# Column tiles for the dense work that follows a visit of values

## The chip, the cores and the metric

The kernel runs on one core of a Trainium2 chip. The metric is the device time of one execution in microseconds. Before the change the median of three runs is 562.47 us (562.46 to 562.88).

## What is computed

Two layers of attention with a memory (A), each followed by a feed-forward block (B), on 2048 tokens of width 640, in bf16:

```
x = x + A(layernorm(x));  x = x + B(layernorm(x))      # twice, the same weights
A:  q, k, v = x @ wq, x @ wk, x @ wv                   # 32 heads of 20, 4 segments of 512 tokens
    for each segment s:
        p     = softmax(q_s k_s^T / sqrt(20) + causal mask)
        a_dot = p @ v_s
        a_mem = phi(q_s) @ M / (phi(q_s) @ z + 1e-6)   # phi(t) = t + 1 where t > 0, else exp(t)
        o_s   = g * a_mem + (1 - g) * a_dot            # g = sigmoid(beta), per head
        M, z += phi(k_s)^T @ v_s, sum phi(k_s)
    out = o @ wo
B:  out = relu(x @ w1) @ w2                            # 640 to 1728 to 640
```

## The kernel before

The kernel is written by a planner. Every piece of work is a stream: a Python generator that yields operations (scores, exponentials, causal masks, values, transposes, projections, the memory's reads and writes, the feed-forward block, loads). An operation names its engine, the time that the planner holds that engine for it, the semaphores it waits for and the PSUM bank or buffer that it needs. `Sched.run` takes from all streams the operation that can start first by its own clock, with priorities, and appends it to the list of its engine; each engine then works through its list in that order. Everything is unrolled. The plan is made 48 times with slightly different prices for a switch of TensorE (around 97 ns), and the plan with the shortest modelled time is emitted.

TensorE works in three forms. The planner calls them modes and adds 97 ns (`SWITCH_NS`) where an operation's mode differs from that of the one before.

- "rows", the scores (L1114): four heads at once, each head's 20 features in a row tile of 32 partitions, 4 or 8 matmuls in each of the two score buffers. ScalarE takes the exponential of a buffer in one instruction of 1024 columns (L1166), GpSimd cuts the diagonal blocks (L1178).
- "cols", the values: `apply` (L1257) multiplies the probabilities of one group of four heads with the values. Four column tiles of 32 stand side by side, one for each head, and four steps of 512, 384, 256 and 128 columns follow each other, so 16 matmuls, called a visit here. There are 60 of them; four more groups (m of 2 and 3) are worked token by token, in the whole-array form (L1208). The last 64 hidden features of a feed-forward block (`ffn_last`, L1405) also have this mode; they use two column tiles of 64, for two halves of the tokens, and 10 matmuls.
- "full", all else: dense matmuls through the helper `group` (L651 the first of a group, L654 the others): the projections of q, k (512 columns, one chunk of 128 features) and v (320), the output projection (320), the first (512) and second (320) matmul of the feed-forward block. The memory's read (L1007, groups of three matmuls of 147 or 84 columns) and its write (L1058, 147 or 168 columns) are in this form too.

The scores pace the attention: between two rounds of them, some 2 to 3 us apart, the planner fills TensorE's list with a visit where one is due, and with whatever dense work is ready. An operation of mode "cols" that would follow whole-array work is held back by up to 4 us (`JOIN_NS`), so that it may come right behind a round of scores. Scores, visits and dense work wait for ScalarE, VectorE, GpSimd and the DMA queues by semaphores; SP issues the transfers, among them the transposes.

Of the kernel before, what the change touches and what calls it, by code (L numbers as in the profile page):

```python
# [16 lines left out]
DFF = 1728  # L17
# [96 lines left out]
class Op:  # L114
# [1 line left out]

    def __init__(self, alts, waits, dma=None, acq=None, urgent=False, take=(), mode="full"):
        self.alts = alts  # L120
        self.mode = mode
# [55 lines left out]
class Sched:  # L177
# [72 lines left out]
    def _pick(self, slots):  # L250
        return min((s for s in slots if s.free), default=None,
                   key=lambda s: max([self.at(t) for t in s.tks], default=0.0))

    def _alts(self, op):
        res = []
        waits = op.waits
        if op.acq is not None:
            s = self._pick(op.acq)
            if s is None:
                return res  # L260
            waits = waits + s.tks
        for k, (e, hold, fns, tail) in enumerate(op.alts):
            m = PE_MARGIN if e == "pe" else 0.0
            if e == "pe" and op.mode != self.pe_mode:
                hold = hold + self.switch
            start = max([self.at(t) + SEM_NS + m for t in waits], default=0.0)
            start = max(self.free[e], start)
            res.append((start + hold, start, k, e))
        return res

    def run(self):
        while True:
# [50 lines left out]
                    str(getattr(st[2], "key", None) or [s.name for s in st[2].slots][:2]) for st in stuck))  # L323
            _, st, end, start, k, op = best
            e, hold, fns, tail = op.alts[k]
            waits, slot = op.waits, None
            for s in op.take:
                s.free = False
# [4 lines left out]
                fns = [(lambda eng, fn=fn, slot=slot: fn(eng, slot), mark) for fn, mark in fns]  # L333
            if e == "pe":
                self.keep_busy(op, start)
                if op.mode != self.pe_mode:
                    hold = hold + SWITCH_NS
            self.P.waits(e, waits)
            self.free[e] = end
            if e == "pe":  # L340
                self.pe_mode = op.mode
            if op.dma is not None:
                tk = self.P.dma(e, fns[0][0], op.dma)
                self.dma_free = max(self.dma_free, start + 300.0) + tail[1]
# [40 lines left out]
        return max(t.values())  # L385


def pe(ns, fns, waits=(), acq=None, take=(), mode="full"):
    return Op([("pe", ns, fns, 190.0)], waits, acq=acq, take=take, mode=mode)


def mm_ns(n):
# [26 lines left out]
def plan(switch, sb, sem_, psum, dram, A_x, A_wq, A_wk, A_wv, A_wo, A_beta, B_x, B_w1, B_w2, out):  # L419
# [224 lines left out]
    def group(slots, n, mms, waits):  # L644

        bk = tk = None
        last = len(mms) - 1
        for k, (a, b, *w) in enumerate(mms):
            w = list(w[0]) if w else []
            if k == 0:  # L650
                bk, tk = yield pe(mm_ns(n), [(lambda e, bk, a=a, b=b: e.matmul(  # L651
                    bk.ap[:, 0:n] if len(b.shape) == 2 else bk.ap[:, 0:n].rearrange("p (i n) -> p i n", n=128), a, b, start=True, stop=(last == 0)), last == 0)], list(waits) + w, acq=slots)
            else:
                tk = yield pe(mm_ns(n), [(lambda e, k=k, a=a, b=b, bk=bk: e.matmul(  # L654
                    bk.ap[:, 0:n] if len(b.shape) == 2 else bk.ap[:, 0:n].rearrange("p (i n) -> p i n", n=128), a, b, start=False, stop=(k == last)), k == last)], w)
        return bk, tk


# [335 lines left out]
    def mem_read(hb):  # L994
        def f(a, s):
            if s == 0:
                return
            phi = yield Need("phi", a, s)
            bdt = yield Need("BD", a, s - 1)
            yield Acq([OMS[hb]])  # L1000
            wr = []
            lst = [(c, max(CH_H0[c], 16 * hb), min(CH_H1[c], 16 * hb + 16)) for c in range(FC)]
            lst = [x for x in lst if x[1] < x[2]]
            for i in range(NJ):
                fns = []
                for z, (c, h0, h1) in enumerate(lst):
                    fns.append((lambda e, bk, c=c, h0=h0, h1=h1, z=z, i=i: e.matmul(  # L1007
                        bk.ap[:, (h0 - 16 * hb) * 21:(h1 - 16 * hb) * 21],
                        STGS[sx(a, s)][:, c, 1, i * 128:(i + 1) * 128],
                        BD[:, CH_OFF[c] + (h0 - CH_H0[c]) * 21:CH_OFF[c] + (h1 - CH_H0[c]) * 21],  # L1010
                        start=(z == 0), stop=True, skip_group_check=True), z == len(lst) - 1))
                bk, tk = yield pe(60.0 * len(lst), fns, phi + bdt, acq=MISC[:1])
# [31 lines left out]
    def mem_write(a, s):  # L1044
        mg = yield Need("maskg")
        if s < NSEG - 1:
            vt = yield Need("v", a, s)
            upd = []
            lastd = None
            for p, cs in enumerate(PARTS):  # L1050
                pht = yield Need("phkT", a, s, p)
                o0 = CH_OFF[cs[0]]
                w = CH_OFF[cs[-1] + 1] - o0
                bk = None
                for i in range(NJ):
                    fns = []
                    for c in cs:
                        fns.append((lambda e, b=None, c=c, i=i, o0=o0, st=(i == 0 and c == cs[0]), bk=bk: e.matmul(  # L1058
                            (b or bk).ap[:, CH_OFF[c] - o0:CH_OFF[c + 1] - o0], phk[:, c, i, :],
                            VAUG[vx(a, s)][:, i, CH_H0[c]:CH_H1[c], :].rearrange("p h e -> p (h e)"),  # L1060
                            start=st, stop=True, skip_group_check=True), i == NJ - 1 and c == cs[-1]))
                    if i == 0:
                        bk, lastd = yield pe(66.0 * len(cs), fns, pht + vt, acq=MISC)
                    else:
                        lastd = yield pe(66.0 * len(cs), fns)
# [330 lines left out]
    def ffn_last(b, s):  # L1396
# [5 lines left out]
        fns = []  # L1402
        for k in range(FC):
            for z in range(2):
                fns.append((lambda e, bk, k=k, z=z: e.matmul(  # L1405
                    bk.ap[64 * z:64 * z + 64, 0:256].rearrange("p (i n) -> p i n", n=128),
                    w1_r[:, k, NFULL * 128:DFF], feat(xt, k)[:, 2 * z:2 * z + 2],
                    start=(k == 0), stop=(k == FC - 1)), k == FC - 1 and z == 1))
# [168 lines left out]
```

## Time and profile before

| | |
|---|---|
| median of three runs | 562.47 us |
| the profiled execution: its own time | 562.46 us |
| its span, first to last instruction | 560.6 us |
| TensorE: busy, matmuls | 555.5 us (99%), 5110 |
| weight loads: busy, number | 302.6 us (54%), 5111 |
| VectorE, ScalarE: busy | 410.8 us, 409.7 us (73% each) |
| GpSimd: busy | 194.3 us (35%) |
| chain that ended last: share of TensorE | 90% |
| granted TensorE clock | 1.00 |

The groups are named by line, engine, operation, what is written and read, and the shape: `128*32 128x512` is a matmul with 128 rows and 32 columns of the array that streams 512 columns, `20*128` a row tile, `128*128` the whole array. In the order of time each row has the start, the time to the end of the last of its instructions, and the number of them (x16); instructions of neighbouring lines of the same helper are merged. TensorE's matmuls overlap, and the end of each is modelled, so distances between starts say more than the lengths of the records: a matmul of 512 columns has a record of some 380 ns, and the next one starts long before it is over.

### The profile page before, as it was taken

Reading aid. Unit: us, or ns where it says so; the run is one execution under the profiler, and the core shown is the slowest. Engines: PE = TensorE matmul, PEld = TensorE weight load, DVE = VectorE, ACT = ScalarE, POOL = GpSimd, SP = SyncE. Lnnn points to the kernel's source line nnn. Section 1 sums busy time; section 2 is a strip of 40 time slices with the busy share of each in tenths; the row PEclk is TensorE's granted clock in tenths of the full one; section 3 lists DMA queues with packets and bytes.
Section 4 is the critical chain, followed back from the end, with each engine's and each line's share of the span. In section 5 each row is a group of like instructions: output and inputs, shape, how many; then the busy total and the mean of one; then the engine's idle time right before and its main releaser. Section 6 shows DMA issues by size and latency. Waiting matters only on the chain.

```text
span 560.6 us, 12651 instructions
## 1 busy us (share of the span) xinstructions
PE 555.5 (99%) x5110; PEld 302.6 (54%) x5111; DVE 410.8 (73%) x1060; ACT 409.7 (73%) x522; POOL 194.3 (35%) x302
## 2 busy tenths in 40 slices
PE   8999999999999999999999999999999999999998
PEld 7654545545644455645356554465445654665655
DVE  5898899776998787877888987889824866651202
ACT  5799999987699779787897789877856788323140
POOL 4534344333354444344433443335401433100000
DMA  8599988741374137443373505550325510422101
GB/s 269 118 201 219 254 202 164 172 123 44 90 175 99 50 89 185 88 99 79 97 179 52 127 20 137 131 120 20 67 77 154 114 43 20 93 69 55 41 1 47
DMA packets 132219, 61.43 MB, mean 110 GB/s; under 512 B 111042, under 2 KB 122050, under 8 KB 132162
## 3 DMA queue, kind: packets, MB, share of 16 engines
q1 hardware_dynamic: 131942, 60.37, 45.7%
q8 instruction: 40, 0.66, 0.5%
q10 hardware_dynamic: 220, 0.26, 0.2%
q14 instruction: 17, 0.14, 0.1%
HBM read 20.57 MB, written 12.85 MB: 60 GB/s over the span
## 4 chain that ended last, share of the span: by engine, by line
PE 90%; DVE 8%; DMA 1%; ACT 0%; POOL 0%; issue 0%
PE ps L654 58%; PE ps L651 12%; PE ps L1114 9%; PE ps L1257 7%; DVE stats L662 2%; PE ps L1058 2%; PE ps L1007 2%; DVE x_sb L1328 1%; PE ps L1405 1%; DVE stg L827 1%; DMA x_sb<-in_A_x_dram 1%; DVE xn_tok L704 1%; DVE av L1265 0%; DVE xn_tok L716 0%; DVE mv L664 0%; ACT PT L1166 0%
## 5 line engine op out<-in xcount | busy, mean ns | idle before, releaser
L1166 ACT ACTIVATE PT<-ps 128x1024 bf16<-128x1024 f32 x320 | 310.1, 1022 | 66.1 <-PE ps L1114 64.5
L1178 POOL TENSOR_SCALAR_AFFINE_SELECT PT<-PT 128x512 bf16<-128x512 bf16 x256 | 166.3, 668 | 267.7 <-ACT PT L1166 267.7
L654 PE MATMUL ps<-w_r,hT 128*128 128x320 bf16 (+2 forms) x768 | 123.4, 299 | 0.1
L654 PE MATMUL ps<-xnT,w_r 128*128 128x512 bf16 x416 | 113.6, 379 | 0.0
L1328 DVE TENSOR_TENSOR x_sb<-x_sb,ps 128x320 bf16<-128x320 bf16 (+1 forms) x128 | 60.4, 479 | 70.2 <-PE ps L654 69.9
L654 PEld LDWEIGHTS ps<-w_r,hT 128*128 128x128 bf16 x768 | 72.2, 98 | 34.2 <-issue 6.3
L1436 ACT ACTIVATE hT<-ps 128x512 bf16<-128x512 f32 x55 | 33.0, 599 | 46.4 <-PE ps L654 46.1
L1114 PE MATMUL ps<-pad 20*128 20x384 bf16 (+3 forms) x1024 | 64.9, 301 | 0.0
L654 PEld LDWEIGHTS ps<-xnT,w_r 128*128 128x128 bf16 x416 | 39.7, 98 | 42.1 <-issue 2.9
L662 DVE BATCH_NORM_STATS2 stats<-x_sb 128x6 f32<-128x320 bf16 x126 | 55.9, 470 | 2.3 <-DMA x_sb<-in_A_x_dram 2.0
L1265 DVE CAST av<-ps 128x512 bf16<-128x512 f32 x56 | 38.3, 684 | 12.9 <-PE ps L1257 12.5
L1114 PEld LDWEIGHTS ps<-pad 20*128 20x128 bf16 x1024 | 18.2, 92 | 51.4 <-ACT PT L1166 24.2
L654 PE MATMUL ps<-wo_r,oT 128*128 128x320 bf16 x256 | 45.3, 299 | 0.0
L1434 DVE TENSOR_SCALAR hT<-ps 128x512 bf16<-128x512 f32 x49 | 33.5, 684 | 10.5 <-PE ps L654 10.0
L1257 PE MATMUL ps<-PT,v_aug 128*32 128x256 bf16 (+5 forms) x896 | 40.7, 302 | 0.0
L651 PE MATMUL ps<-xnT,w_r 128*128 128x512 bf16 x104 | 39.6, 381 | 0.0
L654 PE MATMUL ps<-wv_r,xnT 128*128 128x320 bf16 x192 | 35.8, 300 | 0.0
L654 PE MATMUL ps<-xnT,wk_r 128*128 128x512 bf16 (+1 forms) x140 | 35.5, 349 | 0.0
L676 POOL TENSOR_TENSOR rstd<-lnU,mhalf 128x2 f32<-128x2 f32 (+2 forms) x25 | 20.3, 811 | 39.9 <-DVE lnU L672 39.7
L654 PE MATMUL ps<-xnT,wq_r 128*128 128x512 bf16 (+1 forms) x140 | 33.9, 349 | 0.0
L1301 DVE TENSOR_TENSOR o_sb<-avt,rden 128x320 bf16<-128x320 bf16 x60 | 33.3, 572 | 0.7
L654 PEld LDWEIGHTS ps<-wo_r,oT 128*128 128x128 bf16 x256 | 24.8, 98 | 11.3 <-issue 1.3
(120 smaller groups left out, 686.9 us busy)
## 6 DMA issues: line engine op xcount, KB each, us to landing
pad<-scr SPq DMA_DIRECT2D x124, 80.0 KB
scr<-stg SPq DMA_DIRECT2D x34, 256.0 KB, 2.9
out_dram<-x_sb SPq DMA_DIRECT2D x15, 160.0 KB, 1.8
w_r<-in_B_w_dram SPq DMA_DIRECT2D x10, 216.0 KB, 3.3
w_r<-in_B_w_dram SPq DMA_DIRECT2D x13, 160.0 KB, 2.7
x_sb<-in_A_x_dram SPq DMA_DIRECT2D x9, 160.0 KB, 3.3
scr<-w_r SPq DMA_DIRECT2D x5, 256.0 KB, 3.5
x_sb<-in_A_x_dram SPq DMA_DIRECT2D x3, 320.0 KB, 7.3
```

The lines of the kernel that those rows point to most:

```text
L651: bk, tk = yield pe(mm_ns(n), [(lambda e, bk, a=a, b=b: e.matmul(bk.ap[:, 0:n] if len(b.shape) == 2 else bk.ap[:, 0:n].rearrange("p (i n) ...
L654: tk = yield pe(mm_ns(n), [(lambda e, k=k, a=a, b=b, bk=bk: e.matmul(bk.ap[:, 0:n] if len(b.shape) == 2 else bk.ap[:, 0:n].rearrange("p (i ...
L662: tk = yield dve(320, 1, lambda e, c2=c2: e.bn_stats(stats6[:, t, c2, :], x_sb[:, t, c2 * 320:(c2 + 1) * 320]), xt)
L1114: fns.append([(lambda e, z=z, j=j, hh=hh, N=N, o=o, sl=sl: e.matmul(ps[:, hh, o:o + N], sl.ap[32 * hh:32 * hh + DH, z, 0, 128 * j:128 * j ...
L1166: tx = yield act(1024, lambda e, dst=dst, src=src: e.activation(dst, src, ACT.Exp, scale=SCALE), sc + pw)
L1178: tm = yield pool(600.0, lambda e, reg=reg: e.affine_select(out=reg, in_=reg, pattern=[[0, 4], [1, 128]], compare_op=ALU.is_ge, fill=0.0, ...
L1257: fns.append((lambda e, bk, j=j, hh=hh, pt=pt, g=g0 + z: e.matmul(bk.ap[32 * hh:32 * hh + wide(g, hh), 128 * j:L], VAUG[vx(a, s)][:, j].re ...
L1265: te = yield evac(L, 1, lambda e, sl=sl, z=z, bk=bk: e.tensor_copy(sl.ap[:, z], bk.ap), lambda e, sl=sl, z=z, bk=bk: e.activation(sl.ap[:, ...
L1301: to = yield dve(320, 1, lambda e, dst=dst, src=src, rz=rz: e.tensor_tensor(dst, src, rz, ALU.mult), [tg] + OSB.tks)
L1328: ta = yield dve(n, 1, lambda e: e.tensor_tensor(x_sb[:, t, c0:c0 + n], x_sb[:, t, c0:c0 + n], bk.ap[:, 0:n], ALU.add), [tk] + list(waits) ...
L1434: th = yield evac(512, 1, lambda e, dc=dc, bk=bk: e.tensor_scalar(hT[:, dc, :], bk.ap[:, :], 0.0, None, ALU.max), lambda e, dc=dc, bk=bk: ...
L1436: lambda e, dc=dc, bk=bk: e.activation(hT[:, dc, :], bk.ap[:, :], ACT.Relu), [tk] + HT.tks)
```

## The change

An operation of TensorE may now carry a second list of instructions, `cols`, and a surcharge, `cols_ns`. The new method `mode_of` decides between them when the operation is placed: if TensorE is in mode "cols" and the stream of scores has not ended, an operation that has such a list is emitted as column tiles and leaves the mode as it is; otherwise it is emitted as before. Dense matmuls, the memory's reads and its writes get the list: each matmul becomes four with 32 columns of the weights each, which write the four quarters of the partitions of the same bank and stream the same columns. Only the last of the four of a group's last matmul signals its semaphore. For the planner's clock the dense matmuls keep their price, those of the memory get 45 ns more each. Transposes and the values by token have no such list. `ffn_last` always uses four column tiles of 32 in place of two of 64.

```diff
+    def mode_of(self, op):
+        return "cols" if op.cols is not None and self.pe_mode in ("cols",) and not self.streams[0][4] else op.mode
...
-            if e == "pe" and op.mode != self.pe_mode:
+            if e == "pe" and self.mode_of(op) != self.pe_mode:
                 hold = hold + self.switch
+            if e == "pe" and op.cols is not None and self.mode_of(op) != op.mode:
+                hold = hold + op.cols_ns
...
+            mode = self.mode_of(op)
+            if e == "pe" and mode != op.mode:
+                fns = op.cols
...
             if e == "pe":
-                self.pe_mode = op.mode
+                self.pe_mode = mode
...
+            def whole(e, bk, k=k, a=a, b=b, wide=wide):
+                return e.matmul(to(bk.ap, wide), a, b, start=(k == 0), stop=(k == last))
+
+            def tile(e, bk, y, k=k, a=a, b=b, wide=wide):
+                return e.matmul(to(bk.ap[32 * y:32 * y + 32], wide), a[:, 32 * y:32 * y + 32], b,
+                                start=(k == 0), stop=(k == last))
...
-                tk = yield pe(mm_ns(n), [(lambda e, k=k, a=a, b=b, bk=bk: e.matmul(
-                    bk.ap[:, 0:n] if len(b.shape) == 2 else bk.ap[:, 0:n].rearrange("p (i n) -> p i n", n=128), a, b, start=False, stop=(k == last)), k == last)], w)
+                tk = yield pe(mm_ns(n), [(lambda e, bk=bk, whole=whole: whole(e, bk), k == last)], w, cols=[
+                    (lambda e, y=y, bk=bk, tile=tile: tile(e, bk, y), k == last and y == 3) for y in range(4)])
...
+                bk, tk = yield pe(60.0 * len(lst), fns, phi + bdt, acq=MISC[:1], cols=cols, cols_ns=45.0 * len(lst))
...
+                    more = dict(cols=cols, cols_ns=45.0 * len(cs))
...
             for z in range(2):
-                fns.append((lambda e, bk, k=k, z=z: e.matmul(
-                    bk.ap[64 * z:64 * z + 64, 0:256].rearrange("p (i n) -> p i n", n=128),
-                    w1_r[:, k, NFULL * 128:DFF], feat(xt, k)[:, 2 * z:2 * z + 2],
-                    start=(k == 0), stop=(k == FC - 1)), k == FC - 1 and z == 1))
+                for y in range(2):
+                    fns.append((lambda e, bk, k=k, z=z, y=y: e.matmul(
+                        bk.ap[64 * z + 32 * y:64 * z + 32 * y + 32, 0:256].rearrange("p (i n) -> p i n", n=128),
+                        w1_r[:, k, NFULL * 128 + 32 * y:NFULL * 128 + 32 * y + 32], feat(xt, k)[:, 2 * z:2 * z + 2],
+                        start=(k == 0), stop=(k == FC - 1)), k == FC - 1 and (z, y) == (1, 1)))
```

More of the change, by code (lines that the diff above doesn't have):

```diff
@@ L114, with __init__ @@
 class Op:
-    def __init__(self, alts, waits, dma=None, acq=None, urgent=False, take=(), mode="full"):
+    def __init__(self, alts, waits, dma=None, acq=None, urgent=False, take=(), mode="full", cols=None, cols_ns=0.0):
         self.alts = alts
+        self.cols = cols
+        self.cols_ns = cols_ns
         self.mode = mode
@@ L335, in run @@
                 self.keep_busy(op, start)
-                if op.mode != self.pe_mode:
+                if mode != self.pe_mode:
                     hold = hold + SWITCH_NS
+                if mode != op.mode:
+                    hold = hold + op.cols_ns
             self.P.waits(e, waits)
@@ L385, in late, with pe @@
         return max(t.values())
-def pe(ns, fns, waits=(), acq=None, take=(), mode="full"):
-    return Op([("pe", ns, fns, 190.0)], waits, acq=acq, take=take, mode=mode)
+def pe(ns, fns, waits=(), acq=None, take=(), mode="full", cols=None, cols_ns=0.0):
+    return Op([("pe", ns, fns, 190.0)], waits, acq=acq, take=take, mode=mode, cols=cols, cols_ns=cols_ns)
 def mm_ns(n):
@@ L647, in group, with to @@
         last = len(mms) - 1
+        def to(ap, wide):
+            return ap[:, 0:n] if wide else ap[:, 0:n].rearrange("p (i n) -> p i n", n=128)
         for k, (a, b, *w) in enumerate(mms):
             w = list(w[0]) if w else []
+            wide = len(b.shape) == 2
+            def whole(e, bk, k=k, a=a, b=b, wide=wide):
[3 more added lines that the diff above has]
+                                start=(k == 0), stop=(k == last))
             if k == 0:
-                bk, tk = yield pe(mm_ns(n), [(lambda e, bk, a=a, b=b: e.matmul(
-                    bk.ap[:, 0:n] if len(b.shape) == 2 else bk.ap[:, 0:n].rearrange("p (i n) -> p i n", n=128), a, b, start=True, stop=(last == 0)), last == 0)], list(waits) + w, acq=slots)
-            else:
-                tk = yield pe(mm_ns(n), [(lambda e, k=k, a=a, b=b, bk=bk: e.matmul(
-                    bk.ap[:, 0:n] if len(b.shape) == 2 else bk.ap[:, 0:n].rearrange("p (i n) -> p i n", n=128), a, b, start=False, stop=(k == last)), k == last)], w)
+                bk, tk = yield pe(mm_ns(n), [(whole, last == 0)], list(waits) + w, acq=slots, cols=[
+                    (lambda e, bk, y=y, tile=tile: tile(e, bk, y), last == 0 and y == 3) for y in range(4)])
+            else:
+                tk = yield pe(mm_ns(n), [(lambda e, bk=bk, whole=whole: whole(e, bk), k == last)], w, cols=[
+                    (lambda e, y=y, bk=bk, tile=tile: tile(e, bk, y), k == last and y == 3) for y in range(4)])
         return bk, tk
@@ L1005, in f, with read @@
                 fns = []
-                for z, (c, h0, h1) in enumerate(lst):
[L1007 to L1012, printed above, removed]
+                cols = []
+                def read(e, bk, c, h0, h1, z, p0, p1, i=i):
+                    return e.matmul(
+                        bk.ap[p0:p1, (h0 - 16 * hb) * 21:(h1 - 16 * hb) * 21],
+                        STGS[sx(a, s)][:, c, 1, i * 128 + p0:i * 128 + p1],
+                        BD[:, CH_OFF[c] + (h0 - CH_H0[c]) * 21:CH_OFF[c] + (h1 - CH_H0[c]) * 21],
+                        start=(z == 0), stop=True, skip_group_check=True)
+                for z, (c, h0, h1) in enumerate(lst):
+                    fns.append((lambda e, bk, k=(c, h0, h1, z), read=read: read(e, bk, *k, 0, 128), z == len(lst) - 1))
+                    for y in range(4):
+                        cols.append((lambda e, bk, k=(c, h0, h1, z), read=read, y=y: read(
+                            e, bk, *k, 32 * y, 32 * y + 32), z == len(lst) - 1 and y == 3))
+                bk, tk = yield pe(60.0 * len(lst), fns, phi + bdt, acq=MISC[:1], cols=cols, cols_ns=45.0 * len(lst))
                 rm = yield Acq(RMEM[hb])
@@ L1056, in mem_write, with write @@
                     fns = []
-                    for c in cs:
[L1058 to L1061, printed above, removed]
+                    cols = []
+                    def write(e, b, c, p0, p1, i=i, o0=o0, cs=cs, bk=bk):
+                        return e.matmul(
+                            (b or bk).ap[p0:p1, CH_OFF[c] - o0:CH_OFF[c + 1] - o0], phk[:, c, i, p0:p1],
+                            VAUG[vx(a, s)][:, i, CH_H0[c]:CH_H1[c], :].rearrange("p h e -> p (h e)"),
+                            start=(i == 0 and c == cs[0]), stop=True, skip_group_check=True)
+                    for c in cs:
+                        end = i == NJ - 1 and c == cs[-1]
+                        fns.append((lambda e, b=None, c=c, write=write: write(e, b, c, 0, 128), end))
+                        for y in range(4):
+                            cols.append((lambda e, b=None, c=c, y=y, write=write: write(
+                                e, b, c, 32 * y, 32 * y + 32), end and y == 3))
+                    more = dict(cols=cols, cols_ns=45.0 * len(cs))
                     if i == 0:
-                        bk, lastd = yield pe(66.0 * len(cs), fns, pht + vt, acq=MISC)
+                        bk, lastd = yield pe(66.0 * len(cs), fns, pht + vt, acq=MISC, **more)
                     else:
-                        lastd = yield pe(66.0 * len(cs), fns)
+                        lastd = yield pe(66.0 * len(cs), fns, **more)
                 if s == 0:
```

## The prediction

> **What bounds the kernel now.** I read the page's first two parts, then the busy time by stretch, then the groups of TensorE by shape, and last the order of time around single visits of values. The page and the stretches first.
>
> ```profile
> span 560.6 us, 12651 instructions
> PE 555.5 (99%) x5110; PEld 302.6 (54%) x5111; DVE 410.8 (73%) x1060; ACT 409.7 (73%) x522; POOL 194.3 (35%) x302
> 19.47:479.00 459.53, 458.90 (x4417) 239.81 (x4416) 374.94 (x965) 380.81 (x470) 181.93 (x275) 1.00 0.50 116
> 480.00:561.00 81.00, 78.23 (x518) 47.54 (x517) 22.91 (x56) 18.07 (x31) 2.75 (x4) 1.00 0.19 49
> ```
>
> The columns of the last two are the stretch, its length, the busy time (and count) of TensorE, its weight loads, VectorE, ScalarE and GpSimd, then the granted clock, the DMA share and GB/s. From the first scores (19.47 us) to the last (479.0) TensorE lacks 459.53 - 458.90 = 0.63 us of being always busy, at clock 1.00, while ScalarE and VectorE are busy for 381 and 375 of 460 us. So in this stage the time is the length of TensorE's own list, and what shortens that list shortens the run as long as the others keep up. A busy TensorE is not one at its peak, though: the order of time shows what lies between the matmuls.
>
> ```profile
> 168.61 0.39 PE L651 MATMUL ps<-xnT,w_r 128*128 128x512 bf16 x1
> 168.84 1.03 PE L654 MATMUL ps<-xnT,w_r 128*128 128x512 bf16 x4
> ...
> 254.57 0.38 PE L654 MATMUL ps<-xnT,wk_r 128*128 128x512 bf16 x1
> 254.79 0.38 PE L651 MATMUL ps<-xnT,wq_r 128*128 128x512 bf16 x1
> 255.00 0.30 PE L651 MATMUL ps<-wo_r,oT 128*128 128x320 bf16 x1
> 255.14 0.71 PE L654 MATMUL ps<-wo_r,oT 128*128 128x320 bf16 x4
> 255.78 0.40 PE L1114 MATMUL ps<-pad 20*128 20x384 bf16 x8
> 256.11 0.73 PE L1257 MATMUL ps<-PT,v_aug 128*32 128x512 bf16 x16
> 256.77 0.31 PE L651 MATMUL ps<-wo_r,oT 128*128 128x320 bf16 x1
> 256.91 0.71 PE L654 MATMUL ps<-wo_r,oT 128*128 128x320 bf16 x4
> 257.46 0.30 PE L651 MATMUL ps<-wo_r,oT 128*128 128x320 bf16 x1
> ```
>
> The first number is the start. Whole-array matmuls follow each other at their column count: 512 columns in 0.216 us (254.57 to 254.79 to 255.00), 320 in 0.136 (256.91 to 257.46 is four), so 0.425 ns a column. Scores (L1114) use row tiles, values (L1257) four column tiles of 32, dense work the whole array. A price shows at each border. The fourth matmul of the row at 255.14 starts at 255.55 and would be through at 255.68, but the scores start at 255.78: 0.10 us. The visit of values holds 16 matmuls, four abreast of 512, 384, 256 and 128 columns, 1280 columns in all, 1280 x 0.425 = 0.544 us; it takes 256.77 - 256.11 = 0.66, again 0.12 more. And the first matmul behind a border keeps the next one waiting a little longer: 168.61, behind a visit, to 168.84 is 0.23 where the cadence is 0.216; I take 0.010.
>
> **Part 1: the switch behind a visit goes.** The groups by shape give the number of visits: the 512-column matmuls of L1257, four to a visit.
>
> ```profile
> L1257 PE MATMUL ps<-PT,v_aug 128*32 128x512 bf16 x217 | 22.4, 390 | 0.0
> L1257 PE MATMUL ps<-PT,v_aug 128*21 128x512 bf16 x7 | 2.7, 385 | 0.0
> L1257 PE MATMUL ps<-PT,w_r 128*32 128x512 bf16 x16 | 1.6, 390 | 0.0
> ```
>
> (217 + 7 + 16) / 4 = 60 visits. Reading their followers in the order of time, 59 go on to whole-array work, and two of these come after the last scores, where the new code leaves everything whole. So 57 borders go, from the first of these rows to the last:
>
> ```profile
> 29.33 0.73 PE L1257 MATMUL ps<-PT,w_r 128*32 128x512 bf16 x16
> 29.99 0.45 PE L654 MATMUL ps<-wv_r,hT 128*128 128x320 bf16 x2
> ...
> 470.81 0.73 PE L1257 MATMUL ps<-PT,v_aug 128*32 128x512 bf16 x16
> 471.47 0.39 PE L651 MATMUL ps<-xnT,w_r 128*128 128x512 bf16 x1
> ```
>
> Each saves 0.116 at the border (0.66 - 0.544) and 0.010 behind it. Two bits of this stay: the visit's own first step, behind the scores, has 0.010 as well, and I leave another 0.010 to a tiled stretch for its end, since four tiles that start one after the other also end so. 0.126 - 0.020 = 0.106, and 57 x 0.106 = 6.0 us. The border in front of the next scores stays (column tiles to row tiles now); 0.10 us is what every kind of border in these rows costs.
>
> **Part 2: the last hidden chunk.** L1405 now runs two tiles of 64 columns and becomes four of 32, the form of the values, so that it can stand behind a visit without a border.
>
> ```profile
> 169.79 0.74 PE L1405 MATMUL ps<-xnT,w_r 128*64 128x256 bf16 x10
> 170.46 0.40 PE L1114 MATMUL ps<-pad 20*128 20x512 bf16 x4
> ```
>
> Ten matmuls, two abreast, are 5 x 256 x 0.425 = 0.544 us and take 0.67; the same columns four abreast take the same (a visit has 256 in one of its steps). Of the eight such blocks five are next to work of the visit's form before scores (this is one: the rows from 168.61 stand behind a visit and run up to it) and lose one border each; one more visit stands behind dense work that an earlier visit has left in column form. 6 x 0.106 = 0.6 us.
>
> **Part 3: the dense matmuls themselves.** I count 341 of 320 columns and 269 of 512 between those 57 visits and the next scores. Each becomes four matmuls and four loads. I take +0: the visit does just this, sixteen loads of 32 columns and sixteen matmuls in 0.66 us with nothing to spare between its steps. What hides the four loads is the streaming before, 0.136 or 0.216 us. If that cover is not enough, the bound from the same rows is the 0.010 that a first matmul pays: 610 x 0.010 = 6.1 us. The lower end is 0; no row has column tiles faster than the whole array.
>
> **Part 4: the memory's matmuls.** These are short, and here four instructions in place of one can show. Behind visits stand 48 of L1007 (16 groups of three) and 31 of L1058.
>
> ```profile
> 82.65 0.34 PE L1007 MATMUL ps<-BD,w_r 128*128 128x84 bf16 x3
> 82.83 0.38 PE L638 MATMUL ps<-ident 128*128 128x128 bf16 x4
> ...
> 119.13 0.34 PE L1007 MATMUL ps<-BD,stg 128*128 128x147 bf16 x3
> 119.31 0.59 PE L654 MATMUL ps<-xnT,w_r 128*128 128x512 bf16 x2
> ...
> 231.36 0.69 PE L1058 MATMUL ps<-v_aug,phk 128*128 128x147 bf16 x8
> 231.89 0.57 PE L654 MATMUL ps<-w_r,hT 128*128 128x320 bf16 x3
> ...
> 457.75 0.35 PE L1007 MATMUL ps<-BD,stg 128*128 128x147 bf16 x3
> 457.93 0.38 PE L651 MATMUL ps<-xnT,w_r 128*128 128x512 bf16 x1
> ```
>
> Now a group of L1007 (147, 147 and 84 columns) takes 0.18 us and one of L1058 0.53 / 8 = 0.066. No row has four abreast of so few columns, so I bound it. Below: if streaming sets the pace, +0. Above: the 256-column step of L1405 does two loads of 64 columns and two matmuls in 0.109, so four abreast take at most about that: 16 x (3 x 0.109 - 0.18) + 31 x (0.109 - 0.066) = 2.4 + 1.3 = 3.7 us. The nearest row is that of very short matmuls, each with its own load:
>
> ```profile
> 75.35:76.35 1.00, 1.00 (x42) 1.00 1.02 373
> 54.19:64.19 10.00, 10.00 (x153) 1.00 0.95 227
> ```
>
> In the microsecond from 75.35 TensorE starts a new one of L1208 (21 columns) every 0.025 us (40 of the 42 are its). Four such pairs are 0.100: 16 x (0.300 - 0.18) + 31 x (0.100 - 0.066) = 1.9 + 1.1 = 3.0 us. I take 3.0.
>
> The Trainium skill has a rule that speaks against the change at this place: "TensorEngine Tiling (Array Packing)", section "Restrictions and Gotchas", says that column tiling cannot be had together with the fast weight load, and "TensorE: Matmul & The Clock Gate", section "LDWEIGHTS", prices a plain load at its columns over 1.2 GHz, which by my estimate is 27 ns for 32 columns and 107 for four in a row. By that the memory's matmuls would cost 16 x (0.321 - 0.18) + 31 x (0.107 - 0.066) = 3.5 us and the sum would be 0.5 us worse; the dense ones would still cover their loads, and the records cannot tell, since they give a load of 128 columns (L654) and one of 32 (L1257) nearly the same length:
>
> ```profile
> L654 PEld LDWEIGHTS ps<-wo_r,oT 128*128 128x128 bf16 x256 | 24.8, 98 | 11.3 <-issue 1.3
> L1257 PEld LDWEIGHTS ps<-PT,v_aug 128*32 128x32 bf16 x868 | 18.9, 96 | 21.1 <-POOL PT L1178 6.3 <-issue 5.3 <-DVE rtmp L967 0.3
> ```
>
> **What else moves.** No wait, DMA or buffer is added: the waits stay on the first tile, the semaphore on the last. The order is made anew by the planner, which now sees a different price list; nothing here tells its choice, so I enter 0 and bound it by the waits TensorE has today, 0.6 us between 19.47 and 479.0, up to 2 more. ScalarE and VectorE have 79 and 85 us to spare in that stage, so 1% less from TensorE does not make them late on average.
>
> **The sum.** -6.0 - 0.6 + 0 + 3.0 = -3.6 us on the profiled execution: its span 560.6 becomes 557.0, its own time 562.46 becomes 558.9. The median of the runs is 562.47, the same; so 558.9.
>
> **Rivals.**
> - New waits take it back. For: the margin is 3.6 us, and the plan keeps the list full only because each wait was placed; one more stage in which a visit or an exponential comes late costs 0.3 to 0.5 us, and ten would do. Against: 0.63 us of such gaps in 460 us now. Time: 562.5.
> - Dense tiles lose a little each. It decides from 3.6 / 610 = 0.006 us per matmul; with the 0.010 above the time is 558.9 + 6.1 = 565.0. Against: the steps inside a visit, which fit 0.544 us.
> - TensorE's instruction supply (the case on the other side). Between the scores at 255.78 and those at 261.25 stand one visit and eleven dense matmuls behind it:
>
> ```profile
> 255.78:261.25 5.47, 5.47 (x63) 1.00 0.29 70
> ```
>
> 63 matmuls become 63 + 33 = 96 in 5.36 us, 0.056 apiece, and each brings a load. The densest ten microseconds of today (54.19 on) hold 153, 0.065 apiece. If that were the supply's limit, the cycle would take 96 x 0.065 = 6.28 us, 0.81 more than now, and 57 of them 46: 608 us. It decides from 0.056. Against: one microsecond at 0.025, though a queue filled beforehand could feed so short a burst. The section "Wait — 56ns, not 53.3ns?" of the Trainium skill's "TensorE: Matmul & The Clock Gate" names 62 ns per matmul where firmware decodes them, and none where hardware does; by the 62 the cycle would be 5.95 us and the kernel 562.5 + 57 x 0.48 = 590. The rows neither show nor exclude it.
>
> **How the numbers follow.** My forecast has 0.72, with a range of its own from 555.3 (memory at no price, some borders more) to 561.6 (memory at its upper bound and two microseconds of new waits). New waits 0.12, dense tiles 0.08, the supply 0.08. The range 555.3 to 564.5 leaves out the supply and half of the dense-tile case and a little below. A measurement of this kernel can tell about 0.2%, 1.1 us. Faster: 0.72 less the edge of it, 0.71. Same: most of the new waits, 0.11. Slower: dense tiles, supply and the rest of the waits, 0.18.
>
> **What would show it.** In the changed profile the matmuls number about 5110 + 3 x 689 + 80 = 7260; L651 and L654 appear with the 128*32 form; a row of L1257 is followed by dense tiles 0.55 us later in place of 0.66; dense tiles of 320 columns come every 0.136 us per four; L1007 and L1058 in that form every 0.100 per four. The prediction is wrong if the fours of dense work stand further apart than the whole matmuls do, if TensorE lacks more than 2 us of the stage, or if the planner moves many more than 79 memory matmuls behind visits (each group of three costs 0.12, more than the border).

## The result, and the profile after

The changed kernel takes 568.77 us (median of six, 566.18 to 571.54) against 562.62 for the kernel before in the same comparison: a ratio of 1.0111, interval 1.0096 to 1.0126. It is slower, where the prediction had 558.9. The profiled execution took 568.70 us, its span is 566.9.

The page of the changed kernel (first two parts and the granted clock), then its busy time by stretch, with the columns as in the prediction: the stage from the first to the last scores, what follows, and one short stretch.

```profile
span 566.9 us, 16787 instructions
PE 555.3 (98%) x7176; PEld 312.4 (55%) x7176; DVE 412.6 (73%) x1064; ACT 407.2 (72%) x518; POOL 193.5 (34%) x302
...
PEclk9999989999999999999999999999999999999999
...
19.50:482.20 462.70, 456.03 (x6439) 247.80 (x6438) 374.33 (x965) 377.91 (x466) 180.70 (x275) 0.99 0.53 115
482.20:567.00 84.80, 82.37 (x586) 50.24 (x578) 26.30 (x62) 19.21 (x32) 3.25 (x5) 1.00 0.20 50
75.00:89.00 14.00, 12.12 (x136) 6.97 (x136) 9.55 (x28) 9.98 (x13) 5.63 (x9) 0.76 0.86 189
```

The matmuls number 7176, near the 7260 foretold, so the tiles are there. But in the stage of the scores TensorE now lacks 462.70 - 456.03 = 6.67 us, where it lacked 0.63; the stage is 3.2 us longer (462.7 against 459.5), and the time after the last scores is 3.1 us longer (84.7 against 81.6). And there is a stretch of 14 us in which the granted clock is 0.76.

The order of time shows that the tiles themselves do what they should. A visit with a group of memory reads behind it, a visit with dense work of 512 columns behind it, and dense work of 320 columns:

```profile
117.05 0.73 PE L1300 MATMUL ps<-PT,v_aug 128*32 128x512 bf16 x16
117.60 0.34 PE L1034 MATMUL ps<-BD,stg 128*32 128x147 bf16 x12
117.77 1.47 PE L672 MATMUL ps<-xnT,w_r 128*32 128x512 bf16 x24
...
272.67 0.73 PE L1300 MATMUL ps<-PT,v_aug 128*32 128x512 bf16 x16
273.22 1.25 PE L672 MATMUL ps<-xnT,wk_r 128*32 128x512 bf16 x20
274.30 0.61 PE L672 MATMUL ps<-xnT,wq_r 128*32 128x512 bf16 x8
...
320.34 0.85 PE L672 MATMUL ps<-wo_r,oT 128*32 128x320 bf16 x20
321.02 0.39 PE L672 MATMUL ps<-xnT,w_r 128*32 128x512 bf16 x4
```

The visit gives way after 0.55 us in place of 0.66; five dense fours of 512 columns take 274.30 - 273.22 = 1.08, 0.216 each, and five of 320 columns 321.02 - 320.34 = 0.68, 0.136 each, as whole ones did; three memory reads take 0.17 as fours of tiles, where they took 0.18 whole. Reading the order of all matmuls, I count 347 borders between forms where there were 405 (tiles of 64 columns counted as a form of their own).

What is new are waits. From the list of TensorE's waits (each row ends with the total in us, the number and the longest), and the first of the long ones in the order of time:

```profile
PE ps L1034 <- DVE w_r L1000: 1.4, 1, 1.4
PE ps L669 <- DVE v_aug L903: 1.4, 1, 1.4
PE ps L1157 <- ACT PT L1209: 1.2, 2, 0.9
...
PE ps L672 <- DVE av L1308: 0.8, 2, 0.4
PE ps L669 <- DMA xnT<-xn_tok: 0.5, 1, 0.5
...
76.91 1.16 PE L1251 MATMUL ps<-w_r,PT 128*128 128x21 bf16 x40 [0.45 <-POOL PT L1221]
78.00 0.40 PE L1157 MATMUL ps<-pad 20*128 20x384 bf16 x8
79.83 0.34 PE L1034 MATMUL ps<-BD,w_r 128*128 128x84 bf16 x3 [1.43 <-DVE w_r L1000]
80.01 1.00 PE L650 MATMUL ps<-ident 128*128 128x128 bf16 x15
...
85.87 2.47 PE L669 MATMUL ps<-wv_r,xnT 128*128 128x320 bf16 x10
```

The number in brackets is the idle time and who ended it. Behind the two at 77 and 79.8 the clock falls: ten matmuls of 320 columns from 85.87 spread over 2.47 us, where they need 1.5 at full clock.

### The profile page after: what moved, and what is told of

Its sections match the earlier page's. It is cut to its first block, busy times and chain, and to the rows that moved or that the text cites. A ratio compares the mean times of both kernels' runs of the same rounds, so it can differ in the third digit from the quotient of the medians.

```text
span 566.9 us, 16787 instructions
## 1 busy us (share of the span) xinstructions
PE 555.3 (98%) x7176; PEld 312.4 (55%) x7176; DVE 412.6 (73%) x1064; ACT 407.2 (72%) x518; POOL 193.5 (34%) x302
## 4 chain that ended last, share of the span: by engine, by line
PE 71%; DVE 19%; ACT 4%; DMA 3%; issue 1%; POOL 1%; SPq 0%
PE ps L669 42%; PE ps L672 13%; PE ps L1157 7%; PE ps L1300 5%; DVE stats L687 3%; ACT PT L1209 3%; DMA avt<-av 2%; DVE x_sb L1371 2%; DVE o_sb L1344 2%; DVE xn_tok L741 1%; PE ps L1034 1%; DVE stg L852 1%; DVE av L1308 1%; DVE hT L1478 1%; DVE xn_tok L729 1%; DVE rtmp L992 1%
## 5 line engine op out<-in xcount | busy, mean ns | idle before, releaser
L669 PE MATMUL ps<-w_r,hT 128*128 128x320 bf16 (+2 forms) x676 | 104.8, 299 | 0.0
L669 PE MATMUL ps<-xnT,w_r 128*128 128x512 bf16 x368 | 87.7, 380 | 0.0
L669 PEld LDWEIGHTS ps<-w_r,hT 128*128 128x128 bf16 x676 | 63.8, 98 | 29.7 <-issue 4.1
L1157 PE MATMUL ps<-pad 20*128 20x512 bf16 (+3 forms) x1024 | 65.7, 303 | 1.3 <-ACT PT L1209 1.2
L669 PEld LDWEIGHTS ps<-xnT,w_r 128*128 128x128 bf16 x368 | 34.1, 98 | 40.0 <-issue 4.9
L1300 PE MATMUL ps<-PT,v_aug 128*32 128x128 bf16 (+4 forms) x896 | 40.7, 302 | 0.0
L672 PE MATMUL ps<-xnT,w_r 128*32 128x512 bf16 x608 | 38.5, 379 | 0.0
L852 DVE CAST stg<-ps 128x512 bf16<-128x512 f32 (+1 forms) x46 | 28.7, 630 | 10.1 <-PE ps L672 5.9
L669 PE MATMUL ps<-wo_r,oT 128*128 128x320 bf16 x218 | 35.7, 300 | 0.0
L1300 PEld LDWEIGHTS ps<-PT,v_aug 128*32 128x32 bf16 (+1 forms) x896 | 19.2, 96 | 21.1 <-issue 6.4
```

The lines of the kernel that those rows point to most:

```text
L669: return e.matmul(to(bk.ap, wide), a, b, start=(k == 0), stop=(k == last))
L672: return e.matmul(to(bk.ap[32 * y:32 * y + 32], wide), a[:, 32 * y:32 * y + 32], b, start=(k == 0), stop=(k == last))
L852: te = yield evac(N, 1, lambda e, sg=sg, bk=bk: e.tensor_copy(sg.ap[:, t0:t0 + N], bk.ap[:, 0:N]), lambda e, sg=sg, bk=bk: e.activation(sg ...
L1157: fns.append([(lambda e, z=z, j=j, hh=hh, N=N, o=o, sl=sl: e.matmul(ps[:, hh, o:o + N], sl.ap[32 * hh:32 * hh + DH, z, 0, 128 * j:128 * j ...
L1300: fns.append((lambda e, bk, j=j, hh=hh, pt=pt, g=g0 + z: e.matmul(bk.ap[32 * hh:32 * hh + wide(g, hh), 128 * j:L], VAUG[vx(a, s)][:, j].re ...
```

## The experiments

Four theories were held against each other. A: the tiles save what was forecast, and the new order of the work loses more. B: the tiled form itself loses. C: even the old order gives no more than a little, since it is balanced at TensorE's present length. E: what a new order costs is the draw of the plan, whatever the change. (D is the rival of C in its own experiment.)

**The old order with the new forms.** The planner keeps to the old rule, so the order of all instructions is that of before; only what is emitted follows the form that TensorE is really in.

```diff
...
     def mode_of(self, op):
-        return "cols" if op.cols is not None and self.pe_mode in ("cols",) and not self.streams[0][4] else op.mode
+        return op.mode
...
-            if e == "pe" and mode != op.mode:
-                fns = op.cols
+            if e == "pe":
+                tiled = op.cols is not None and self.form == "cols" and not self.streams[0][4]
+                self.form = "cols" if tiled else op.mode
+                fns = op.cols if tiled else fns
```

> The order of all instructions is that of the kernel before; only the form changes: dense and memory matmuls behind a visit are emitted as column tiles, ffn_last as four tiles of 32. Theory A (the new order opens waits, the tiles themselves do what they should): some 63 borders at 0.106 us go and the memory's matmuls cost nothing (66 ns per four of 147 columns in the changed kernel's trace), so 562.6 - 6.7 = about 556 us, TensorE's waits in the attention stage stay under 2 us. Theory B (the tiled form itself is what costs, by supply or by loads): 562.6 + 6 = 568 to 569 us, with TensorE spread out and no waits on other engines.

Measured: 561.59 us against 562.77, ratio 0.9976 (0.9967 to 0.9985). The sign is A's, the size is nobody's: 1.2 us of the 6.7 that A forecast arrive. The busy time of its stage of scores, and VectorE's list of waits:

```profile
19.88:478.90 459.02, 454.17 (x6577) 247.64 (x6576) 373.33 (x965) 380.28 (x470) 182.51 (x275) 1.00 0.55 117
...
DVE rden L1339 <- DMA avt<-av: 10.1, 9, 2.4
```

TensorE's work in the stage is 4.7 us shorter than before (454.17 against 458.90) and the stage 0.5 us shorter (459.02 against 459.53): TensorE lacks 4.85 us where it lacked 0.63. One place shows how. VectorE's list holds the division of a visit, which needs the visit's transposed copy, ahead of the evacuation of projected values; the next visit of TensorE needs those values. The order of time of VectorE, then of TensorE:

```profile
331.24 0.35 DVE L1339 RECIPROCAL rden<-avt 128x32 f32<-128x32 bf16 x1 [2.38 <-DMA avt<-av]
...
333.11 0.48 DVE L906 CAST v_aug<-ps 128x320 bf16<-128x320 f32 x1
...
332.23 0.40 PE L1160 MATMUL ps<-pad 20*128 20x384 bf16 x8
333.74 0.73 PE L1303 MATMUL ps<-PT,v_aug 128*32 128x512 bf16 x16 [1.11 <-DVE v_aug L906]
```

In the kernel before, VectorE stood 0.23 us for this transfer, and 1.8 us for all of them, against 10.1 now:

```profile
330.04 0.35 DVE L1293 RECIPROCAL rden<-avt 128x32 f32<-128x32 bf16 x1 [0.23 <-DMA avt<-av]
...
DVE rden L1293 <- DMA avt<-av: 1.8, 4, 0.7
```

**The new order with whole-array forms.** The changed kernel without the two lines that exchange the instructions (`if e == "pe" and mode != op.mode: fns = op.cols`); the chunk of 64 features stays in four tiles.

> The order of the changed kernel with every dense and memory matmul in whole-array form again (ffn_last stays at four tiles of 32). Theory A (order): the waits of the changed kernel are there or partly covered, and some 58 borders come back: 569 to 575 us, slower than before although no dense matmul is tiled. Theory B (tiles): 562.6, as before, or a little less.

Measured: 570.98 us, ratio 1.0146 (1.0109 to 1.0183). No dense matmul is tiled and the kernel is slower still. So the new order costs some 8 us, of which a part is a lowered clock: the two executions with a granted clock of 1.000 took 568.79 and 569.23, 6.0 and 6.5 us more than before. The tiles take 2.2 us back in the median (570.98 to 568.77), with ranges that overlap, and 2.6 or more at clock 1.000, where the changed kernel took 566.18. This goes against B.

**The last chunk alone.** The kernel before with the chunk's four tiles of 32 in place of two of 64, the last hunk of the diff.

> The kernel before with one change: ffn_last writes four column tiles of 32 in place of two of 64. Its price in the planner is the same, so the order is the old one. Both theories: one border between a visit and such a block goes (0.1 us), the 40 pairs of 256 columns keep their 0.109 us: 562.5, the same. If four tiles of 32 were slower than two of 64, 8 blocks of 5 steps would show it: 1 us for each 25 ns a step.

Measured: 563.39 against 562.77, ratio 1.0015 (1.0005 to 1.0024). The change in the form has no visible price in the trace (a block takes 0.662 us where it took 0.669); the profiled execution differs by waits at the start of the kernel (1.9 us for the first normalised rows against 0.6) and at 324 and 371 us. I read it as no gain, and the 0.6 us as not explained.

**No surcharge.** `cols_ns=0.0` in both places; the planner makes a new plan.

> The changed kernel with the planner's surcharge for tiled memory matmuls set from 45 ns to 0, the price that the changed kernel's trace shows (147 columns: 66 ns per four, as whole). The plan is a new one. Theory A in the form that the surcharge misled the planner: most of the waits go, 556 to 560 us. Theory A in the form that any new plan has its own waits: 560 to 570, with waits at other places. Theory B (tiles): 568 or more.

Measured: 567.66 us, ratio 1.0079 (1.0052 to 1.0106). Setting the price right does not bring the time back by itself. The plan has new waits at other places, and the two of 0.45 and 1.43 us near 77 and 80 us stand in it as in the changed kernel, with a lowered clock behind them. Of its five executions two had a granted clock of 1.000 (564.18 and 566.95 us), the others 0.991 to 0.994 (567.66 to 569.03).

**The old order with more work.** The counterpart of the first experiment: two idle matmuls behind each of 59 visits or chunks.

```diff
...
+                self.seen = op.mode == "cols" or (self.seen and op.mode != "rows")
+                if self.seen and op.mode == "full" and slot is not None and not self.streams[0][4]:
+                    self.seen = False
...
+                    for _ in range(2):
+                        self.P.op("pe", lambda eng, ap=slot.ap: self.idle_fn(eng, ap), False)
```

> The kernel before, order and forms unchanged, with two idle matmuls of 128 columns (2 x 0.056 us, into the bank that the next group has just taken) behind each of 59 visits or chunk blocks before the next scores: 6.6 us more on TensorE's list, the counterpart of the 6.7 us that the run with the old order took off and of which 1.2 arrived. Theory C (the old order is balanced: every other engine's piece is due just when TensorE gets there, so that TensorE's list is the bound only from its present length upwards): nearly all of it arrives, 568 to 569 us, and TensorE waits for others no more than before. Theory D (the other engines' chains were the bound all along and TensorE merely keeps step): a good part is absorbed, 563 to 566.

Measured: 569.39 us against 562.85, ratio 1.0109 (1.0086 to 1.0131). 6.5 of the 6.6 us arrive. Its stage of scores:

```profile
19.38:485.80 466.42, 465.31 (x4535) 246.68 (x4534) 375.48 (x965) 381.64 (x470) 180.05 (x275) 1.00 0.52 114
```

TensorE lacks 1.11 us of 466. So TensorE's list is the bound when it grows by 6.6 us, and nearly not when it shrinks by 6.7. This is what C says; D falls, since little is absorbed.

**Kept warm.** The changed kernel with 20 idle matmuls ahead of the first memory read of each half in segment 1, where the trace has 1.43 us of idle time.

```diff
...
+            if e == "pe" and op.warm:
+                self.P.waits(e, slot.tks)
+                for _ in range(op.warm):
+                    self.P.op("pe", lambda eng, ap=slot.ap: self.idle_fn(eng, ap), False)
...
```

> The changed kernel with 20 idle matmuls ahead of the first memory read of segment 1 of each half (before its wait for phi, where the trace has TensorE idle for 1.43 us at 78.4 us and a granted clock of 0.76 between 75 and 89 us). The order is the changed kernel's. If the lowered clock is a part of the loss: clock 1.000 in the records, no spread of several us between the executions, and the time of the one execution of the changed kernel that had clock 1.000, 566.2 us. If it is not: 568.8 again.

Measured: 568.79 us, ratio 1.0098 (1.0069 to 1.0127): nothing gained, although the early stretch now runs at full clock. The scores that came at 88.44 us come at 85.96, 2.5 us sooner; then VectorE's list stands before the next transposed visit.

```profile
85.96 0.40 PE L1164 MATMUL ps<-pad 20*128 20x384 bf16 x8
...
183.95 0.35 DVE L1343 RECIPROCAL rden<-avt 128x32 f32<-128x32 bf16 x1 [3.45 <-DMA avt<-av]
...
185.66 0.49 DVE L908 CAST v_aug<-ps 128x320 bf16<-128x320 f32 x1
...
PE ps L674 <- DVE v_aug L908: 3.2, 2, 2.8
```

At 183 us TensorE waits 2.8 us for the evacuation behind that division (in the changed kernel 1.4 at this place), and the clock falls there instead. Ahead of this wait the scores were 1.7 us sooner than in the changed kernel (180.88 against 182.54), behind it 0.24. So the time gained in one place was given back 95 us later. What the lowered clock costs by itself this run does not show, since it came again at another place.

**Another plan of the kernel before.** No edit but the list of switch prices: `STARTS = [90.25]`, its planner's second choice.

> The kernel before without any edit but the list of switch prices, which holds 90.25 ns alone: the plan that its planner held second best of 48 (it models 557.6 us to the last event against 552.2 for the one in use). Theory E (what a new plan costs is the draw among plans, whatever the change): 566 to 569 us, as bad as the changed kernel with no tile in it. If plans hardly differ on the chip: 562 to 564.

Measured: 572.95 us, ratio 1.0164 (1.0132 to 1.0196). The same program in another order loses 10 us (7.5 in the one execution with a granted clock of 1.000, 570.37), more than the change did. This is E, and stronger than expected; but the draw is not blind, since the planner's own clock has this plan 5.4 us longer (557.6 against 552.2).

**Another plan of the changed kernel.** `STARTS = [82.75]`.

> The changed kernel with 82.75 ns as the only switch price: second best by its planner's criterion with late transfers, but 554.4 us to the last event where the plan in use has 557.9. Theory E: 563 to 566 us at full clock, 2 to 4 better than the changed kernel with the same tiles. If the tiles are to blame: 568 or more.

Measured: 564.77 us, ratio 1.0030 (1.0019 to 1.0041): 4.0 us better than the changed kernel with the same kind of tiles. Its ten executions all had a granted clock of 1.000; the changed kernel's one such execution took 566.18, so at full clock the distance is 1.4.

**The shortest plans without surcharge.** As in "No surcharge", with 82.75 and with 83.5 as the only switch price.

> The changed kernel with the surcharge of the tiled memory matmuls at 0 and 82.75 ns as the only switch price: of 48 such plans the shortest to the last event, 549.7 us by its planner (the kernel before has 552.2 and measures 562.6, the changed one 557.9 and 566.2 at full clock, the run with other price 554.4 and 564.8). Theory E (borders saved as forecast, and the draw of the plan on top): the distance of 8 to 10.5 us between plan and chip holds, 558 to 560.5 us, faster than before. If the tiles leave nothing however they are planned: 562 or more.

> The same with 83.5 ns, modelled 550.0 us to the last event. Theory E: 558 to 561 us. Where the two neighbours differ by more than 2 us, the plan's own length does not tell the chip's time to better than that.

Measured: 561.29 us, ratio 0.9970 (0.9954 to 0.9986), and 562.16, ratio 0.9989 (0.9979 to 0.9998). The first is the fastest version with a plan of its own; with the old order's 0.9976 it beats both kernels. Both miss their ranges (558 to 560.5 and 558 to 561): the gain in the plan's own length did not carry over to the chip in full. With the same switch price of 82.75 the plan without surcharge is 3.5 us faster than the one with it (561.29 against 564.77), so the wrong price may have had a part in the loss; one pair of plans does not show it.

**Later transposes in the planner.** No surcharge, `lat=3400.0` in place of 1600 for the visit's transposed copy, switch price 86.5.

> The changed kernel with no surcharge, and with the planner told that a transposed visit lands 1.8 us later (3400 ns in place of 1600 behind its issue), switch price 86.5 ns, modelled 552.4 us to the last event with the later landings in it. In the run with the old order VectorE stood 10.1 us behind these transfers, where the kernel before has 1.8. If that is what turns saved borders into waits: VectorE's wait for avt under 3 us, TensorE's waits under 3 us in the attention stage, 556 to 560 us. If those waits only follow from something else: 560 or more, with TensorE's waits at other releasers.

Measured: 562.33 us, ratio 0.9997 (0.9983 to 1.0011). VectorE's waits for these transfers are gone from its list, and the time is not; TensorE's waits have other releasers:

```profile
PE ps L1157 <- ACT PT L1209: 1.5, 3, 1.0
PE ps L1157 <- DMA pad<-scr: 0.9, 1, 0.9
...
PE ps L669 <- DVE v_aug L903: 0.6, 1, 0.6
...
19.65:479.20 459.55, 455.41 (x6594) 249.46 (x6593) 382.65 (x973) 376.09 (x463) 183.24 (x275) 1.00 0.56 117
```

So the late transposes are one way in which a saved border becomes a wait, and taking them away is not enough.

**The old order with less work and no tiles.** The second matmul of every group of the output projection is left out, so this kernel does not compute the whole projection.

```diff
...
+            elif k == skip:
+                yield pe(mm_ns(n), [], w)
...
```

> The kernel before, in its order and with no column tile added, but the second of the five matmuls is left out of each of the 64 groups of the output projection, so that part of the computation is missing: 64 x 0.136 = 8.7 us less on TensorE's list, of which some 8 groups (1.1 us) stand behind the last scores. Theory C (the order is balanced at TensorE's present length, so what is taken off in the attention stage turns into waits, with tiles or without): the 1.1 us arrive and about a fifth of the other 7.6, 560 to 561 us, and TensorE lacks 4 to 6 us in the attention stage. If it is the tiled form that loses in the run with the old order: 562.8 - 8.7, 554 to 555 us.

Measured: 560.23 us against 562.62, ratio 0.9955 (0.9939 to 0.9972): 2.4 of 8.7 us arrive. The stage of scores:

```profile
19.43:478.40 458.97, 453.89 (x4361) 233.22 (x4360) 374.37 (x965) 380.83 (x470) 180.37 (x275) 1.00 0.53 116
```

TensorE lacks 5.08 us of it and the stage is 0.6 us shorter. The same happens as with the tiles, without a tile. Of the 8.7 us some 1.1 lie behind the last scores, where they should arrive in full, so of the 7.6 in the stage some 1.3 arrive (an estimate from 2.4 - 1.1). The busy time of the stage falls by 5.0 us only where 7.6 us of matmuls are gone; probably some waits are hidden under the records, since one of 320 columns lasts 0.30 us where the pace is 0.136.

The chain of work that ended last moves too. Its shares in the kernel before, then in three runs with the old order (more work, the tiles, less work):

```profile
PE 90%; DVE 8%; DMA 1%; ACT 0%; POOL 0%; issue 0%
...
PE 90%; DVE 7%; DMA 1%; POOL 1%; ACT 0%; issue 0%
...
PE 71%; DVE 18%; DMA 7%; ACT 2%; SPq 1%; issue 1%; POOL 1%
...
PE 78%; DVE 14%; DMA 5%; ACT 1%; issue 1%; SPq 0%; POOL 0%
```

It stays TensorE's where work is added, and goes over to VectorE and the DMA queues in part where work is taken off. C is shown from both sides.

## Why the prediction was wrong

**Part 1 (borders, -6.0) was right as a price and wrong as a gain.** The border goes (0.55 for 0.66), and 58 of 405 are gone. But "what shortens that list shortens the run as long as the others keep up" failed. I took 99% busy for a bound with slack around it on the other engines. It is a balance: other chains end just behind TensorE's, so a list that is full says only that nothing was left uncovered at that length. (That the planner makes it so, by filling up to the next input, is a reading of its code; no run shows it.) That ScalarE and VectorE have some 80 us to spare on average says nothing of the single wait. The opposite experiments give the slope: +6.5 for +6.6 us, -1.2 for the -6.7 of the forecast, and in the stage about -1.3 for -7.6.

**Part 2 (the chunk, -0.6)**: the form costs nothing in the trace. Alone it gained nothing (+0.6 us), but there it removes a single border; in the changed kernel six of the eight blocks run on into column tiles and take 0.556 us where they took 0.669. The price was right, and like that of part 1 it did not become time.

**Part 3 (dense tiles, +0) was right**: 0.216 and 0.136 us per four. The rival of a small loss in each falls.

**Part 4 (the memory's matmuls, +3.0) was wrong by its whole size, on the good side.** Groups of three take 0.17 us in tiles, and 53 of the memory's matmuls are tiled, not the 79 foretold. The lower bound (streaming) was the true one; the row of 21 columns, one load at a time in the whole array, was not like four tiles side by side, whose starts lie some 0.004 us apart. The estimate of 3.5 that the prediction worked out beside it, from the price of a load in the Trainium skill ("TensorE: Matmul & The Clock Gate", section "LDWEIGHTS") and four loads of 32 columns in a row, is further off.

**"What else moves" is the step that failed.** It entered 0 for the new order, bounded by 2 us. The order alone costs 8 us (570.98 with no dense tile, and some of that at a lowered clock); two plans of one and the same kernel lie 10 us apart.

"Nothing here tells its choice" was wrong as well: the planner's own clock does. It puts the last event at 552.2 us before and at 557.9 for the changed kernel (both in the expectations above), 5.7 later; at most 2.4 of that is the surcharge (53 matmuls at 0.045), which the chip does not take. Such a plan can be emitted because the planner does not take the shortest one. It takes the least sum over four replays in which transfers land late at random (`late`). The measured time lies above the modelled one by 10.4 us before, 10.9 in the changed kernel, and 10.4, 11.6, 12.2 and 9.9 in the four other tiled plans whose modelled end the expectations give; only the kernel before with 90.25 ns stands out, with some 15. So the modelled end ranks these plans to about 2 us, with that one exception.

The difference between the two profiled executions can be accounted for so, by estimate and not by experiment: 58 borders of 0.106 off, 6.1 us; 6.0 us more of TensorE's idle time in the stage; a clock of 0.76 over 14 us, 14 x 0.24 = 3.4 us; and 35 idle matmuls more than before (89 against 54, written by the planner where it sees a gap), 2.5 us more busy time. Their rows, before and after:

```profile
L638 PE MATMUL ps<-ident 128*128 128x128 bf16 x54 | 5.0, 231 | 0.1
...
L650 PE MATMUL ps<-ident 128*128 128x128 bf16 x89 | 7.5, 236 | 0.0
```

-6.1 + 6.0 + 3.4 + 2.5 = +5.8, near the +6.3 between the two spans; the terms overlap a little, since the idle matmuls partly run in the low clock.

**The rivals.** "New waits take it back" was the right one by its mechanism, with a chance of 0.12 and a price of 3.6 us; the time came out 9.9 us above the forecast, waits, lowered clock and idle matmuls together. "TensorE's instruction supply" falls: in the ten microseconds from 420.81 the changed kernel starts 220 matmuls, 0.045 apiece, under the 0.056 from which that rival would decide, and under the 0.062 that the prediction worked out beside it.

```profile
420.81:430.81 10.00, 10.00 (x220) 1.00 0.83 196
```

What stays open: which chain holds the stage of scores near 459 us (459.53 before, 459.02, 458.97 and 459.55 in the three runs with 3 to 5 us less busy time on TensorE). Taking one late releaser away, by another plan, brought others, at other engines, so there may be no single one. It was not tried to shorten ScalarE's or VectorE's list.

## What to carry to other kernels

An engine that is 99% busy in a list made to measure is not proof that it alone is the bound. Before pricing a saving there, add the same amount of work and take it away, both in the old order: if only the first shows, the saving has to be paired with a new balance of the others. And where a change makes a planner draw anew, read the modelled end of the new plan against that of the old one, compare the change first in the old order, since the draw can outweigh it, and run more than one plan before judging it.

## What the runs showed of the hardware that was not expected

- Four column tiles of 32 with a load each keep the pace of one whole-array matmul even when short: 147 columns about every 0.066 us, 84 columns every 0.036 to 0.040 (from the starts of the memory's reads and writes; the three of a group of reads take 0.17). Whole, the same matmuls came every 0.066 to 0.069 and 0.037.
- Idle stretches of TensorE of 0.45 and 1.43 us, with 1.5 us of short matmuls and scores between them, were followed by some 7 us at about half the clock (0.50 from 81 to 87 us, 0.76 over the 14 us around). The same pair of waits, with a clock of 0.50 behind it, is in the traces of the new order with whole-array forms and of the run without surcharge; in the run kept warm a clock of 0.50 from 187 to 189 us followed one idle stretch of 2.8 us. That the idle time is the cause was not tested apart. It does not come every time: the six executions of the changed kernel had mean clocks of 0.991 to 1.000 and took 571.54 to 566.18 us in that order, a spread of 5 us, where the kernel before has 0.7 in the same comparison.
